# Logits in two groups a block, inputs split at step 6, the first z sum in the transposes' PSUM tile

## The chip, the cores and the metric

The kernel runs on one core of one Trainium2 chip. The metric is the device time of one execution in microseconds (us); a kernel's time is the median of its runs. Five engines work from queues of their own, each strictly in order: PE (TensorE), DVE (VectorE), ACT (ScalarE), POOL (GpSimd) and SP (SyncE, which here only issues DMAs). They meet at semaphores.

## What is computed

The reference, cut to what matters, with x of 8 x 3072 x 256:

```python
X = np.fft.fft(np.fft.fft(x, axis=1), axis=2).real.reshape(24576, 256)
x = (X @ w_a) * (X @ w_b) @ w_out                  # 256 -> 1536 -> 256
logits = x @ phi                                   # 32 slots
d = softmax(logits, over the tokens)
slots = d.T @ x                                    # 32 x 256
out_slots = relu(slots @ w1[e]) @ w2[e]            # 8 experts, 4 slots each
out = softmax(logits, over the slots) @ out_slots
```

## The kernel before

The program has three stages. `_fft` does the Fourier transforms and prepares the weights. `_main` runs from about 215 us to 1555 us of the profile and is the stage that the change touches; it ends in `tail`, which works out the slots. `_out` multiplies the second softmax with the slots' results and stores 24 MB.

`_main` goes through 24 **blocks** (index k) of 1024 tokens. A block has 12 **steps** (index p, the code's `ft`), one for every 128 of the 1536 hidden features; n = 12 k + p counts all 288. The order on every engine is the order in which this Python code issues the instructions; no scheduler moves anything.

What one step issues, by the lines of the profile:

- `layer1(n)`: twelve fp32r matmuls of 512 columns on PE (L531 to L533), six into the PSUM tiles `s`, six into `d`, each of which exists once. DVE adds a correction to the two `s` (L547, twice) and forms sums and a difference with `d` (L552 to L554). ACT copies one `d` (L551). POOL does the rest: a difference (L556) and two products (L557, L558) that give the tile `g`; in every third block (k % 3 == 2) also a copy of one column (L561). `s_sb`, `pl` and `db` have two buffers each, `g` six.
- `transp(n - 2)`: eight PE transposes of the `g` of two steps ago into the PSUM tile `t` (L579), which ACT copies out to `ring` (L582). `t` exists once, so the next transposes wait for that copy.
- In steps 1, 5 and 9 a **group**: `logits` of four `g` tiles (L590, into `l_ps`), then one `z_part` (L599), a sum of the previous block's `ring` tiles weighted by its exponentials. DVE adds the sum to `acc` (L602). The `z` sums, the transposes `y_ps`, `x_ps` and `c_ps` of the softmax steps and some first-block work share one PSUM tile, `x`.

Softmax work on the previous block is spread over the steps by a table: 

```python
    side = {3: ["d"], 4: ["ct"], 5: ["cm", "sum", 0], 9: ["cs", 1], 10: ["co"]}
```

`"cm"` forms exponentials of the logits over the slots (DVE L643 and L644, ACT L645), `"cs"` normalises them (DVE L650, ACT L651, DVE L652 and L653), `"co"` transposes the result (L658) and SP stores it. `"sum"` is a DVE reduction of the other softmax's exponentials (L625) and a small ACT instruction (L626). A number is a `z_part`: 0 in step 5, 1 in step 9; the third is issued in step 1 of the block after.

In step 9 the next block's inputs are split for the fp32r matmuls (`split_eo`): ACT rounds them to `eoh` (L516), DVE subtracts that from them to give the rest `eol` (L519, an instruction with two inputs of 1024 elements in SBUF). SP loads a block's inputs (L507, L508); its queue also carries the stores of `"co"`, the loads of the last stage's weights `w1` and `w2` during the last block, and one load of `wo` (1.5 MB) at step 12.

## Time and profile before

| | us |
|---|---|
| median of 3 runs | 1669.15 (1666.14 to 1671.22) |
| the profiled execution, its time | 1664.62 |
| its span, first to last instruction | 1662.6 |
| PE busy | 1598.5 (96%) |
| DVE busy | 1391.2 (84%) |
| POOL busy | 1146.9 (69%) |
| ACT busy | 640.8 (39%) |

A timeline row of the profile reads: start in us from the span's start, duration in us, engine, line, operation, the tile written and the tiles read, shapes, and xN for N neighbouring instructions of one kind that were merged; in brackets the idle time of the engine before it and what ended it. Matmul durations overlap, so PE is read from start to start. The trace records each fp32 matmul of L590 and L599 twice.

### The profile page before, as it was taken

Reading aid. Unit: us, or ns where it says so; the run is one execution under the profiler, and the core shown is the slowest. Engines: PE = TensorE matmul, PEld = TensorE weight load, DVE = VectorE, ACT = ScalarE, POOL = GpSimd, SP = SyncE. Lnnn points to the kernel's source line nnn. Section 1 sums busy time; section 2 is a strip of 40 time slices with the busy share of each in tenths; the row PEclk is TensorE's granted clock in tenths of the full one; section 3 lists DMA queues with packets and bytes.
Section 4 is the critical chain, followed back from the end, with each engine's and each line's share of the span. In section 5 each row is a group of like instructions: output and inputs, shape, how many; then the busy total and the mean of one; then the engine's idle time right before and its main releaser. Section 6 shows DMA issues by size and latency. Waiting matters only on the chain.

```text
span 1662.6 us, 28294 instructions
## 1 busy us (share of the span) xinstructions
PE 1598.5 (96%) x10837; PEld 1166.9 (70%) x10837; DVE 1391.2 (84%) x2055; ACT 640.8 (39%) x990; POOL 1146.9 (69%) x992
## 2 busy tenths in 40 slices
PE   5999999999999999999999999999999999999985
PEld 3555578777777777777777777777777777777554
DVE  8999889888888888888888988888888888888633
ACT  1322324434434444434343443433443434434343
POOL 1000069888878887888788778877887788878421
PEclk9999999999999999999999999999999999999975
DMA  9777330000000000000000000000000000002689
GB/s 392 271 249 243 106 98 20 23 1 23 24 23 1 23 23 23 1 23 23 23 1 23 23 20 4 23 23 16 8 23 23 1 23 23 23 1 94 281 338 385
DMA packets 34095, 123.71 MB, mean 74 GB/s; under 512 B 3780, under 2 KB 12035, under 8 KB 26792
## 3 DMA queue, kind: packets, MB, share of 16 engines
q1 hardware_dynamic: 28796, 113.98, 18.7%
q10 hardware_dynamic: 5164, 7.92, 1.3%
q8 instruction: 86, 1.41, 0.4%
q14 instruction: 49, 0.40, 0.1%
HBM read 79.36 MB, written 42.52 MB: 73 GB/s over the span
## 4 chain that ended last, share of the span: by engine, by line
PE 81%; DVE 11%; DMA 4%; issue 2%; ACT 1%; POOL 0%; DVEq 0%; ACTq 0%; SPq 0%
PE t_ps L579 14%; PE s L531 8%; PE d L531 8%; PE d L533 8%; PE d L532 8%; PE s L533 7%; PE s L532 7%; PE l_ps L590 7%; PE z_ps L599 6%; PE pt L262 4%; DMA out_dram<-o 3%; DVE eol L519 2%; PE pt L171 1%; DVE f L269 1%; DVE e L276 1%
## 5 line engine op out<-in xcount | busy, mean ns | idle before, releaser
L556 POOL TENSOR_TENSOR db<-s_sb,db 128x512 f32<-128x512 f32 x287 | 373.0, 1300 | 249.7 <-DVE s_sb L553 99.1
L547 DVE SCALAR_TENSOR_TENSOR s_sb<-ub,w,s 128x512 f32<-128x512 f32 x576 | 404.4, 743 | 72.0 <-PE s L533 69.8
L551 ACT COPY db<-d 128x512 f32<-128x512 f32 x288 | 169.7, 589 | 626.7 <-PE d L533 608.7
L557 POOL TENSOR_TENSOR g<-pl 128x512 f32<-128x512 f32 x288 | 384.9, 1336 | 7.7 <-DVE pl L554 6.9
L558 POOL TENSOR_TENSOR g<-s_sb,db 128x512 f32<-128x512 f32 x287 | 372.4, 1298 | 0.0
L582 ACT COPY ring<-t_ps 128x1024 f32<-128x1024 f32 x286 | 290.5, 1016 | 63.8 <-PE t_ps L579 63.8
L579 PE MATMUL t_ps<-ident,g 128*128 128x128 f32 x2296 | 297.3, 272 | 0.0
L579 PEld LDWEIGHTS t_ps<-ident,g 128*128 128x128 f32 x2296 | 268.3, 140 | 39.3 <-issue 0.4
L531 PE MATMUL s<-eoh,wt 128*128 128x512 f32 x576 | 252.6, 438 | 2.4 <-DVE s_sb L547 2.4
L531 PE MATMUL d<-eoh,wt 128*128 128x512 f32 x576 | 226.9, 394 | 3.1 <-DVE s_sb L553 3.1
L533 PE MATMUL d<-eoh,wt 128*128 128x512 f32 x576 | 227.2, 394 | 0.0
L533 PE MATMUL s<-eoh,wt 128*128 128x512 f32 x576 | 226.5, 393 | 0.0
L532 PE MATMUL s<-eol,wt 128*128 128x512 f32 x576 | 225.2, 391 | 0.0
L532 PE MATMUL d<-eol,wt 128*128 128x512 f32 x576 | 225.1, 391 | 0.0
L553 DVE TENSOR_TENSOR s_sb<-s_sb,d 128x512 f32<-128x512 f32 x288 | 197.8, 687 | 9.9
L554 DVE TENSOR_TENSOR pl<-s_sb,d 128x512 f32<-128x512 f32 x288 | 197.5, 686 | 0.5 <-ACT db L551 0.5
L552 DVE TENSOR_TENSOR pl<-s_sb,d 128x512 f32<-128x512 f32 x288 | 195.6, 679 | 0.0
L531 PEld LDWEIGHTS s<-eoh,wt 128*128 128x128 f32 x576 | 108.4, 188 | 76.1 <-issue 28.9
L590 PE MATMUL l_ps<-g,m_sb 128*32 128x256 f32 x2304 | 139.2, 382 | 0.0
L599 PE MATMUL z_ps<-ring,d_sb 128*32 128x512 f32 x1152 | 136.7, 592 | 0.0
L531 PEld LDWEIGHTS d<-eoh,wt 128*128 128x128 f32 x576 | 108.2, 188 | 30.7 <-DVE s_sb L553 7.6
L533 PEld LDWEIGHTS s<-eoh,wt 128*128 128x128 f32 x576 | 108.1, 188 | 25.0
(186 smaller groups left out, 1699.5 us busy)
## 6 DMA issues: line engine op xcount, KB each, us to landing
out_dram<-o SPq DMA_DIRECT2D x23, 1024.0 KB
xt<-in_x_dram SPq DMA_DIRECT2D x15, 1536.0 KB
eoraw<-eo_c SPq DMA_DIRECT2D x16, 512.0 KB
w2t<-in_moe_w_dram SPq DMA_DIRECT2D x4, 2048.0 KB
w1t<-in_moe_w_dram SPq DMA_DIRECT2D x3, 2048.0 KB
eo<-so SPq DMA_DIRECT2D x16, 256.0 KB
eoraw<-eo SPq DMA_DIRECT2D x8, 512.0 KB
ub<-eo_c SPq DMA_DIRECT2D x16, 256.0 KB
```

The lines of the kernel that those rows point to most:

```text
L531: nc.tensor.matmul(ps_, wt[ft // 4][:, ft % 4, 0, e, ab], h[:, e], start=True, stop=False)
L532: nc.tensor.matmul(ps_, wt[ft // 4][:, ft % 4, 0, e, ab], l[:, e], start=False, stop=False)
L533: nc.tensor.matmul(ps_, wt[ft // 4][:, ft % 4, 1, e, ab], h[:, e], start=False, stop=True)
L547: nc.vector.scalar_tensor_tensor(out=s_sb[:, ab], in0=ub, scalar=w128[:, ab, ft:ft + 1], in1=s_ps[ab], op0=ALU.mult, op1=ALU.add)
L553: nc.vector.tensor_tensor(am, s_sb[:, 0], d_ps[0], ALU.subtract)
L556: eng.tensor_tensor(bm, s_sb[:, 1], db, ALU.subtract)
L557: nc.gpsimd.tensor_tensor(g[:, 0:512], pl[:, 0], pl[:, 1], ALU.mult)
L558: eng.tensor_tensor(g[:, 512:1024], am, bm, ALU.mult)
L579: nc.tensor.transpose(t_ps[:, z], g[:, z * P:z * P + P], ident)
L582: nc.scalar.copy(dst, t_ps)
L590: nc.tensor.matmul(l_ps[k][NS * c:NS * c + NS], m_sb[:, ft], g[:, 256 * c:256 * c + 256], start=(ft == 0), stop=(ft == NFT - 1))
L599: nc.tensor.matmul(z_ps[NS * c:NS * c + NS], d_sb[:, hh, NS * c:NS * c + NS], ring[:, :, 2 * c + hh, :], start=(hh == 0), stop=(hh == 1))
```

## The change

- `logits` are issued in two groups a block: five tiles in step 6 and seven in step 1 of the next block. So that the tiles live long enough `g` has nine buffers; the 12 KB for them come from `wo`, which is no tile of its own any more but three loads into `g` buffers, two in the last step and one in `tail`.
- In step 6 the group stands ahead of the step's transposes, behind the `d` matmuls; in step 1 it stands behind the transposes as before. Both `z` sums 0 and 1 are issued in step 6, one behind the other. Sum 0 takes the PSUM tile `t`, sum 1 the tile `x`.
- The next block's inputs are rounded on ACT in step 5 (`split_h`) and the rest is formed on DVE in step 6 (`split_l`), between `"cm"` and the first `z` sum's addition to `acc`. `"cs"` moves from step 9 to step 6, behind that addition; `"co"` from step 10 to step 8.
- The sum of the exponentials is taken by ACT's exponential itself (`accum_out`), and the DVE reduction L625 is gone.

Line numbers of the changed kernel are higher by one from `layer1` on; L513 and L519 are the two halves of the split there.

```diff
-    gp = ctx.enter_context(tc.tile_pool(reuse_waits="tile", name="m_g", bufs=6))
+    gp = ctx.enter_context(tc.tile_pool(reuse_waits="tile", name="m_g", bufs=9))
...
-            nc.scalar.activation(dt_, l_sb, ACTF.Exp, bias=bm[:, 1:2])
+            nc.scalar.activation(dt_, l_sb, ACTF.Exp, bias=bm[:, 1:2], accum_out=al[:, 1:2])
...
-            nc.vector.tensor_reduce(out=al[:, 1:2], in_=s["dt"], axis=AX.X, op=ALU.add)
...
-    side = {3: ["d"], 4: ["ct"], 5: ["cm", "sum", 0], 9: ["cs", 1], 10: ["co"]}
+    side = {3: ["d"], 4: ["ct"], 5: ["h"], 6: ["cm", "sum", "l", 0, "cs", 1], 8: ["co"]}
...
-                z_part(k, v)
+            elif k >= 0:
+                z_part(k, v, "x" if v else "t")
...
+    def load_wo(q):
+        t = gp.tile([P, 1024], F32, tag="g", name="wo").rearrange("p (t d) -> p t d", t=4)
+        nc.sync.dma_start(t, wof[:, 4 * q:4 * q + 4])
+        wo.append(t)
...
-            if p == 9 and k + 1 < nblk:
-                split_eo(k + 1)
...
-        if n >= 2:
+        if n >= 2 and p != 6 and n <= nper:
             rest = transp(n - 2)
...
-        if n % 4 == 1 and 1 < n < nper:
-            for z in range(5, 1, -1):
+            for z in range(7, 1, -1):
                 logits(n - z)
-        if k > 0 and p == 1:
+        if p == 1 and k > 0:
+            for z in range(8 if n < nper else 2, 1, -1):
+                logits(n - z)
...
+        if p == 6:
+            for z in range(6, 1, -1):
+                logits(n - z)
+        if n == nper - 1:
+            load_wo(0)
+            load_wo(1)
...
+        if p == 6:
+            transp(n - 2)
```

What stands in a row on PE in the middle of the program, before: the end of a step 9, its transposes and its group, and the first matmuls of step 10 (`eoh`, `eol` are the inputs, `wt` the weights, `m_sb` the matrix from hidden features to logits, `d_sb` the exponentials).

```order
L532 MATMUL d_8456<-eol,wt 128x512
L533 MATMUL d_8456<-eoh,wt 128x512
L579 MATMUL t_ps<-ident,g 128x128 x8
L590 MATMUL l_ps<-g,m_sb 32x256 x16
L599 MATMUL z_ps<-ring,d_sb 32x512 x8
L531 MATMUL s_8528<-eoh,wt 128x512
L532 MATMUL s_8528<-eol,wt 128x512
```

And on PE after the change, the end of a step 6 and the beginning of step 7:

```order
L533 MATMUL d_8086<-eol,wt 128x512
L534 MATMUL d_8086<-eoh,wt 128x512
L591 MATMUL l_ps<-g,m_sb 32x256 x20
L600 MATMUL z_ps<-ring,d_sb 32x512 x16
L580 MATMUL t_ps<-ident,g 128x128 x8
L532 MATMUL s_8178<-eoh,wt 128x512
L533 MATMUL s_8178<-eol,wt 128x512
```

The group moved ahead of the transposes, and it holds five tiles' logits and two `z` sums in place of four and one.

On DVE before, the end of step 5 with its softmax work and the beginning of step 6:

```order
L554 TENSOR_TENSOR pl<-s_sb,d_7457 128x512
L643 TENSOR_REDUCE cm<-x_ps 128x8
L644 TENSOR_TENSOR ce<-x_ps,cm 128x256
L625 TENSOR_REDUCE al<-dt 128x1
L602 SCALAR_TENSOR_TENSOR acc<-acc,al,z_ps 128x512
L547 SCALAR_TENSOR_TENSOR s_sb<-ub,w_85,s_7527 128x512
```

On DVE before, four steps later, the end of step 9 and the beginning of step 10:

```order
L554 TENSOR_TENSOR pl<-s_sb,d_7648 128x512
L519 TENSOR_TENSOR eol<-eoraw,eoh 128x1024
L650 TENSOR_REDUCE cs<-ce 128x8
L652 RECIPROCAL cs<-cs 128x8
L653 TENSOR_TENSOR ce<-ce,cs 128x256
L602 SCALAR_TENSOR_TENSOR acc<-acc,al,z_ps 128x512
L547 SCALAR_TENSOR_TENSOR s_sb<-ub,w_85,s_7719 128x512
```

On DVE after the change, the end of step 6 and the beginning of step 7:

```order
L555 TENSOR_TENSOR pl<-s_sb,d_7487 128x512
L643 TENSOR_REDUCE cm<-x_ps 128x8
L644 TENSOR_TENSOR ce<-x_ps,cm 128x256
L519 TENSOR_TENSOR eol<-eoraw,eoh 128x1024
L603 SCALAR_TENSOR_TENSOR acc<-acc,al,z_ps 128x512
L650 TENSOR_REDUCE cs<-ce 128x8
L652 RECIPROCAL cs<-cs 128x8
L653 TENSOR_TENSOR ce<-ce,cs 128x256
L603 SCALAR_TENSOR_TENSOR acc<-acc,al,z_ps 128x512
L548 SCALAR_TENSOR_TENSOR s_sb<-ub,w_85,s_7578 128x512
```

The two pieces of DVE work became one; the subtraction L519 stands where L625 stood, directly ahead of the first addition to `acc`, and steps 5 and 9 hold nothing but their own five instructions.

## Rows read from the trace of the kernel before

**Rows 1.** The page: busy time of each engine, share of the span, instructions.
```profile
PE 1598.5 (96%) x10837; PEld 1166.9 (70%) x10837; DVE 1391.2 (84%) x2055; ACT 640.8 (39%) x990; POOL 1146.9 (69%) x992
```

**Rows 2.** The page: the chain that ended last, shares by engine.
```profile
PE 81%; DVE 11%; DMA 4%; issue 2%; ACT 1%; POOL 0%; DVEq 0%; ACTq 0%; SPq 0%
```

**Rows 3.** Timeline of PE: a step 5 with its group, block 10; last, tail.
```profile
792.81 0.48 PE L531 MATMUL s<-eoh,wt 128*128 128x512 f32 x1
...
795.66 1.04 PE L579 MATMUL t_ps<-ident,g 128*128 128x128 f32 x8
796.63 1.93 PE L590 MATMUL l_ps<-g,m_sb 128*32 128x256 f32 x32
798.38 1.90 PE L599 MATMUL z_ps<-ring,d_sb 128*32 128x512 f32 x16
800.21 0.50 PE L531 MATMUL s<-eoh,wt 128*128 128x512 f32 x1
...
1563.93 3.64 PE L599 MATMUL z_ps<-ring,d_sb 128*32 128x512 f32 x32
```

**Rows 4.** Timeline of PE: first matmuls of steps 10, 11 and 0, block 3.
```profile
425.84 0.50 PE L531 MATMUL s<-eoh,wt 128*128 128x512 f32 x1
...
430.18 0.50 PE L531 MATMUL s<-eoh,wt 128*128 128x512 f32 x1 [0.22 <-DVE s_sb L547]
...
434.46 0.48 PE L531 MATMUL s<-eoh,wt 128*128 128x512 f32 x1
```

**Rows 5.** Timeline of PE: the same three matmuls in block 11.
```profile
875.26 0.50 PE L531 MATMUL s<-eoh,wt 128*128 128x512 f32 x1
...
879.13 0.48 PE L531 MATMUL s<-eoh,wt 128*128 128x512 f32 x1
...
882.77 0.48 PE L531 MATMUL s<-eoh,wt 128*128 128x512 f32 x1
```

**Rows 6.** Timeline of DVE: the split's subtraction in blocks 3, 9, 11 and 19.
```profile
423.11 4.34 DVE L519 TENSOR_TENSOR eol<-eoraw,eoh 128x1024 fp32r<-128x1024 f32 x1 [0.26 <-ACT eoh L516]
...
760.17 1.82 DVE L519 TENSOR_TENSOR eol<-eoraw,eoh 128x1024 fp32r<-128x1024 f32 x1 [0.26 <-ACT eoh L516]
...
872.53 1.22 DVE L519 TENSOR_TENSOR eol<-eoraw,eoh 128x1024 fp32r<-128x1024 f32 x1 [0.26 <-ACT eoh L516]
...
1321.89 4.32 DVE L519 TENSOR_TENSOR eol<-eoraw,eoh 128x1024 fp32r<-128x1024 f32 x1 [0.25 <-ACT eoh L516]
```

**Rows 7.** Timeline of POOL: beside the first two of these (blocks 3 and 9).
```profile
418.82 1.32 POOL L556 TENSOR_TENSOR db<-s_sb,db 128x512 f32<-128x512 f32 x1
...
422.57 1.32 POOL L556 TENSOR_TENSOR db<-s_sb,db 128x512 f32<-128x512 f32 x1
...
425.04 1.32 POOL L558 TENSOR_TENSOR g<-s_sb,db 128x512 f32<-128x512 f32 x1
...
760.84 2.29 POOL L557 TENSOR_TENSOR g<-pl 128x512 f32<-128x512 f32 x1
```

**Rows 8.** The line L653: count, duration ns min/median/max.
```profile
L653 DVE TENSOR_TENSOR ce<-ce,cs x24: 424/482/1016, 314.7 to 1577.7; 128x256 f32<-128x256 f32 x24
```

**Rows 9.** Timelines of DVE and POOL: step 5 of block 10.
```profile
797.94 0.41 DVE L625 TENSOR_REDUCE al<-dt 128x1 f32<-128x256 f32 x1
...
796.59 1.29 POOL L556 TENSOR_TENSOR db<-s_sb,db 128x512 f32<-128x512 f32 x1
```

**Rows 10.** Timelines of PE and POOL: step 5 of block 11, one with L561.
```profile
849.54 0.48 PE L531 MATMUL s<-eoh,wt 128*128 128x512 f32 x1
...
849.95 1.30 POOL L556 TENSOR_TENSOR db<-s_sb,db 128x512 f32<-128x512 f32 x1
...
853.95 1.29 POOL L556 TENSOR_TENSOR db<-s_sb,db 128x512 f32<-128x512 f32 x1
```

**Rows 11.** Stretches: busy us (instructions) by engine, clock, DMA share, GB/s.
```profile
1547.00:1551.00 4.00, 4.00 (x24) 2.44 (x17) 2.71 (x5) 0.00 (x0) 2.76 (x3) 1.00 0.00 0
...
1559.00:1583.00 24.00, 21.08 (x203) 9.51 (x199) 9.02 (x25) 6.95 (x20) 1.77 (x2) 1.00 1.01 418
```

More of the change, by code (lines that the diff above doesn't have):

```diff
@@ L509, in load_eo, with split_h, split_l @@
         eo_t[k] = [raw, ub]
-    def split_eo(k):
-        raw, ub = eo_t[k]
-        l = eh.tile([P, 2, 512], F32R, tag="eol", name="eol")
-        h = eh.tile([P, 2, 512], F32R, tag="eoh", name="eoh")
-        if k:
-            nc.scalar.copy(h, raw)
-        else:
-            nc.vector.tensor_copy(h, raw)
+    def split_h(k):
+        h = eh.tile([P, 2, 512], F32R, tag="eoh", name="eoh")
+        (nc.scalar.copy if k else nc.vector.tensor_copy)(h, eo_t[k][0])
+        eo_t[k].append(h)
+    def split_l(k):
+        raw, ub, h = eo_t[k]
+        l = eh.tile([P, 2, 512], F32R, tag="eol", name="eol")
         nc.vector.tensor_tensor(l, raw, h.bitcast(F32), ALU.subtract)
@@ L522, in _main @@
     load_eo(0)
-    split_eo(0)
+    split_h(0)
+    split_l(0)
     nper = nblk * NFT
@@ L565, in transp @@
         k, ft = divmod(n, NFT)
-        g = g_t[n]
+        g = g_t.pop(n) if ft == 4 else g_t[n]
         if ft % 4 == 0:
@@ L585, in logits @@
         k, ft = divmod(n, NFT)
-        g = g_t[n] if n == nper - 1 else g_t.pop(n)
+        g = g_t[n]
         if ft == 0:
@@ L661, in soft_step @@
             nc.sync.dma_start(csc[:, k], ct)
-    side = {3: ["d"], 4: ["ct"], 5: ["cm", "sum", 0], 9: ["cs", 1], 10: ["co"]}
+    side = {3: ["d"], 4: ["ct"], 5: ["h"], 6: ["cm", "sum", "l", 0, "cs", 1], 8: ["co"]}
     def run_side(k, items):
         for v in items:
-            if isinstance(v, str):
+            if v in ("h", "l"):
+                if k + 2 < nblk:
+                    (split_h if v == "h" else split_l)(k + 2)
+            elif k >= 0 and isinstance(v, str):
                 soft_step(k, v)
-            else:
-                z_part(k, v)
+            elif k >= 0:
+                z_part(k, v, "x" if v else "t")
     ex = {}
@@ L739, in tail @@
         soft_step(k, "sum")
+        load_wo(2)
         load_w2(0)
@@ L785, in slots_b @@
             for c in range(4):
-                nc.tensor.matmul(sip[NS * c:NS * c + NS], zt[q][:, c], wo[:, 4 * q + c],
+                nc.tensor.matmul(sip[NS * c:NS * c + NS], zt[q][:, c], wo[q][:, c],
                                  start=(q == 0), stop=(q == 2))
@@ L864, in _main @@
                                 axis=AX.X, op=ALU.add)
-    wo = wpool.tile([P, NFT, D], F32, name="wo")
+    wo = []
     nc.vector.memset(m_run[0], -3.0e38)
@@ L874, in _main @@
             layer1(n)
-            if p == 9 and k + 1 < nblk:
-                split_eo(k + 1)
             if n < 9:
                 extra(n)
-            if n == NFT:
-                nc.sync.dma_start(wo, wof)
-        if n == nper + 1:
-            for z in range(5, 1, -1):
-                logits(n - z)
-        if n >= 2:
+        if n >= 2 and p != 6 and n <= nper:
             rest = transp(n - 2)
@@ L887, in _main @@
             z_part(nblk - 2, 2)
-        if n % 4 == 1 and 1 < n < nper:
-            for z in range(5, 1, -1):
+            for z in range(7, 1, -1):
                 logits(n - z)
-        if k > 0 and p == 1:
+        if p == 1 and k > 0:
+            for z in range(8 if n < nper else 2, 1, -1):
+                logits(n - z)
             soft_step(k - 1, "l")
@@ L896, in _main @@
                     z_part(k - 2, 2)
-        if k > 0 and n < nper:
+        if p == 6:
[4 more added lines that the diff above has]
+            load_wo(1)
+        if n == nper + 1:
+            rest = transp(n - 2)
+        if n < nper:
             run_side(k - 1, side.get(p, []))
+        if p == 6:
+            transp(n - 2)
         if k == nblk - 1 and p in ahead:
```

## The prediction

> **What bounds the kernel now.** I read the page first: PE is busy for 96% of the span and holds 81% of the chain that ended last [rows 1, 2]. DVE, at 84%, has little room, POOL some. So a gain must come out of PE's own sequence or out of the places where PE waits. For these I read PE's timeline from one step's first `s` matmul to the next one's, over all 24 blocks. A plain step takes 3.64 us (879.13 to 882.77, [rows 5]); a step with a group takes 7.40 (792.81 to 800.21, [rows 3]). PE waits in one place only: in nine of the 24 blocks steps 10 and 11 are long. In block 3 they take 4.34 and 4.28 us [rows 4], in block 11 3.87 and 3.64 [rows 5]: 1.11 us lost, 10.0 us in the nine blocks.
>
> The cause stands on DVE. The subtraction L519 takes 1.22 us where POOL is between two instructions (872.53, [rows 6]). In the nine blocks it takes 4.3 us (423.11 is the first, 1321.89 the ninth, [rows 6]). Beside the first, POOL runs L556, L557 and L558 back to back until 425.04 + 1.32 = 426.36, and L519 ends at 427.45, 1.09 later [rows 6, 7]. In seven blocks like block 9 it ends after 1.82 us, and there POOL's next instruction is the one that is stretched, to 2.29 us [rows 6, 7]. So the two engines exclude each other, and when L519 comes while POOL is busy there is a **draw**: won at POOL's next boundary, or lost until POOL runs dry. Of 16 draws 9 were lost; in the remaining seven splits, those of blocks with L561, DVE came first.
>
> **Parts that save.** 1. The stalls in steps 10 and 11 go, as nothing but the usual five DVE instructions is left in step 9: 9 x 1.11 = 10.0 us. If the split in its new place stalls PE again, that is priced below.
>
> 2. Fewer groups. A group adds 7.40 - 3.64 = 3.76 us. Its logits take 1.75 (796.63 to 798.38, four tiles, 0.44 each); a second `z` sum behind a first adds 3.64 - 1.90 = 1.74 [rows 3]. That leaves 3.76 - 1.75 - 1.74 = 0.27 us for going in and out. Tiles and sums stay the same in number; three groups a block become two. In the new group the logits follow the `d` matmuls and the transposes follow `z`, two orders that the trace of before doesn't show, so its going in and out lies between 0 and twice 0.27; I take 0.16, nearer to the measured 0.27 than to the ends and below it because the transposes lead into the next `s` as in a plain step. Saved per block: 2 x 0.27 - 0.16 = 0.38, with the tail's merged group 24 times: 9.1 us (bounds 0 and 13.0).
>
> 3. Costed at nothing. The removed reduction (0.41 us, [rows 9]) was in a step where DVE waited for PE. The accumulator's price on ACT has no row; it lies between nothing and the 0.41 of the instruction that it replaces, on an engine that is 39% busy [rows 1], two steps ahead of its first reader. The rounding on ACT moves into step 5 between two copies; a step's ACT work stays under 3.64 us. SP: the store of `"co"` and the loads queued behind it are issued two steps earlier, the inputs are needed four steps earlier; with nine steps (33 us) left for 0.75 MB that hides. The load of `wo`: two thirds go out when the DMA engines are idle (1547 to 1551, share 0.00); the last third is ahead of `w2` in a stretch that is full (1.01, 418 GB/s, [rows 11]), so `w2` lands 0.52 MB / 418 GB/s = 1.25 us later. That is the bound if PE has no slack there; I take 0.
>
> Without new stalls: 1664.6 (the profiled execution's time) - 10.0 - 9.1 = **1645.5 us**.
>
> **The part that costs: the split in step 6.** The second addition doesn't matter, the first does. The transposes of step 6 need the tile `t`, which holds `z` sum 0 until DVE's L603 has read it, and L603 now stands behind L519. Times from the step's first `s` matmul:
>
> - PE: the transposes of before stood at +2.85 (795.66 - 792.81, [rows 3]). The logits take their place: five tiles, 2.19; two `z` sums, 3.48; with half of the 0.27 the transposes want to start at +8.65.
> - DVE: L625 came at +5.13 (797.94 - 792.81) in step 5; L519 comes there in step 6.
> - POOL: L556 at +3.78 in step 5 [rows 9]. Its cycle is 422.57 - 418.82 = 3.75 us [rows 7], PE's step 3.64, so one plain step later +3.89. The three instructions last to 3.79 after that (426.36 - 422.57): POOL is dry at +7.68. L519 always meets it busy.
> - A lost draw: L519 ends at 7.68 + 1.09 = +8.77, L603 0.74 later at +9.51: PE stalls 0.86 us. Won at the first or the second boundary (+5.2, +6.4), it ends by +7.5, and L603 is done before +8.65: no stall.
> - Blocks with L561: POOL's cycle is 4.00 (849.95 to 853.95), L556 was at +4.41 in step 5 [rows 10], hence at +4.77; dry at +8.56, L519 done at +9.65, L603 at +10.39: 1.74 us. Before, these blocks had no draw; now they have one.
>
> Block 0 has no `z` sum, so at most 15 x 0.86 + 7 x 1.74 = **25.1 us**. With the share lost before, 9 of 16, it is 14.1: 1645.5 + 14.1 = **1659.6**. That share is a weak number. The 24 runs of the shorter two-input instruction L653 never took over 1.02 us [rows 8], less than one POOL instruction (1.3) and itself: they never lost. And L519 will come within 0.1 us of a boundary in most blocks, where before it came 0.8 ahead. The same timing also repeats every three blocks, so draws go together, and the sum can be far from its middle.
>
> The median of before is 4.5 us above the profiled execution; four more lost draws would give that, but no timed run shows it. I carry no offset in the middle and half of it in the upper end.
>
> **Rivals.**
>
> *All draws won (first come, first served).* The waiting engine gets in when the running POOL instruction ends: L519 is done by +7.5, with L561 at 6.06 + 1.09 = +7.15, and PE never stalls: 1645.5, or 1650 with the offset. For it: seven of 16 draws, and L653. Against it: the nine that waited past two more POOL instructions though they came first [rows 6, 7]. The Trainium skill, "SBUF — State Buffer", section "Who interferes with whom", states this rule: a DVE instruction with two SBUF inputs contends with a GpSimd instruction that reads SBUF, the one that issued first holds the shared pair for its whole length and the other blocks until it is done. The trace agrees on the exclusion and disagrees on the order, by the 4.3 us of L519.
>
> *Nearly all draws lost.* One mechanism: L519 waits for POOL's queue to run dry, ahead of L603, which holds `t`. Price 25.1 us: 1670.6, and with the offset 1675, slower than before. It decides from 19.1 / 25.1 = 76% of the price paid; less is a gain.
>
> *The new group is as dear as its bounds.* If going in and out costs 0.54, part 2 is gone: 1659.6 + 9.1 = 1669, no change.
>
> *POOL becomes the bound.* Steps 7 to 11 have no group now. In every third block POOL falls behind by 4.00 - 3.64 = 0.36 us a step, five steps, and then by 0.11 in steps 0 and 1 of the next: 1.8 to 2.0 us, where before it was 0.63 by step 5 (4.41 - 3.78, [rows 9, 10]). If all that reached PE: 7 x 2.0 = 14 us, 1674; I expect none of it, as `g` is needed two steps after it is begun and step 1's group lets POOL catch up; half of it would give 1667.
>
> **How the numbers follow.** Forecast, draws mixed: 1660, its own range 1651 to 1665, chance 0.45. All won 0.22; nearly all lost 0.15; group as dear 0.10; POOL the bound 0.08. A measurement here can tell about 0.3% from no change, so faster is below 1664.1 and slower above 1674.2. Faster: 0.40 of the forecast, 0.22 all won, 0.04 of the last two: 0.66. Slower: 0.08, half of the case of lost draws with the offset and a little of POOL's. Within 0.3%: 0.26. The range reaches from just above all won, 1647, to all lost with half the offset, 1673.
>
> **What would show it.** Steps 10 and 11 at 3.64 in all blocks (step 8 at 3.87) shows part 1. Step 1 at 8.7 and step 6 at 9.4 to 9.5 where L519 is short shows part 2. L519 near 1.2 to 2.4 us with no idle PE ahead of the transposes of step 6 is a draw won; L519 at 3.6 to 4.5 us with step 6 at 10.3 (11.2 with L561) is one lost. The forecast is wrong if L519's length doesn't decide the length of step 6, if steps 7 to 1 are long in blocks with L561, or if `tail` waits for `wo` or `w2`.

## The result and the profile after

The changed kernel takes 1648.26 us (median, 1646.63 to 1651.03), the kernel before 1669.64 (1666.14 to 1671.22) beside it: a ratio of 0.988, interval 0.986 to 0.989, 21.4 us less. The forecast was 1660 (1647 to 1673): the sign is right and the time lies in the range, near its lower end, but the gain is more than twice the 9 us that lay between the forecast and the 1669.15 of before. The profiled execution took 1647.84 with a span of 1645.8, against 1664.62 and 1662.6 before.

The page of the kernel after, busy time by engine and the shares of the chain that ended last [rows 1, 2]:

```profile
PE 1583.5 (96%) x10837; PEld 1165.0 (71%) x10837; DVE 1360.3 (83%) x2031; ACT 643.8 (39%) x1014; POOL 1154.2 (70%) x992
...
PE 84%; DVE 8%; DMA 4%; issue 2%; ACT 1%; POOL 1%; ACTq 0%; SPq 0%; DVEq 0%; POOLq 0%
```

PE is the bound as before. DVE's 24 reductions are gone, and its share of the chain fell from 11% to 8%.

Timeline of PE after, block 3: the first `s` matmul of step 6, the last `d` matmul, the group, the transposes, and the first matmuls of steps 7 and 8 (the answer to [rows 3]):

```profile
401.83 0.47 PE L532 MATMUL s<-eoh,wt 128*128 128x512 f32 x1
...
404.44 0.40 PE L534 MATMUL d<-eoh,wt 128*128 128x512 f32 x1
404.76 2.37 PE L591 MATMUL l_ps<-g,m_sb 128*32 128x256 f32 x40
406.94 3.62 PE L600 MATMUL z_ps<-ring,d_sb 128*32 128x512 f32 x32
410.49 1.09 PE L580 MATMUL t_ps<-ident,g 128*128 128x128 f32 x8
411.34 0.48 PE L532 MATMUL s<-eoh,wt 128*128 128x512 f32 x1
...
414.98 0.48 PE L532 MATMUL s<-eoh,wt 128*128 128x512 f32 x1
```

Step 6 takes 411.34 - 401.83 = 9.51 us, step 7 takes 3.64, and no row has idle time in brackets. All of blocks 2 to 22 read like this, 55.25 us each, within 0.01. By steps, in us, from PE's timeline (first `s` matmul to first `s` matmul), a block without a lost draw on either side (step 0 is left out, 3.64 in both):

| step | 1 | 2 | 3 | 4 | 5 | 6 | 7 | 8 | 9 | 10 | 11 | block |
|---|---|---|---|---|---|---|---|---|---|---|---|---|
| before | 7.40 | 3.66 | 3.85 | 3.85 | 7.38 | 3.66 | 3.63 | 3.64 | 7.40 | 3.88 | 3.64 | 55.62 |
| forecast | 8.7 | | | | | 9.4 to 9.5 | | 3.87 | | 3.64 | 3.64 | |
| after | 8.69 | 3.67 | 3.86 | 3.85 | 3.63 | 9.51 | 3.64 | 3.86 | 3.63 | 3.64 | 3.64 | 55.25 |

The subtraction L519 on DVE after (blocks 3, 5 and 7; [rows 6]), behind the first of them the addition L603 that holds the transposes:

```profile
406.94 1.22 DVE L519 TENSOR_TENSOR eol<-eoraw,eoh 128x1024 fp32r<-128x1024 f32 x1
408.91 0.75 DVE L603 SCALAR_TENSOR_TENSOR acc<-acc,al,z_ps 128x512 f32<-128x512 f32 x1 [0.76 <-PE z_ps L600]
...
517.43 2.09 DVE L519 TENSOR_TENSOR eol<-eoraw,eoh 128x1024 fp32r<-128x1024 f32 x1
...
627.93 2.40 DVE L519 TENSOR_TENSOR eol<-eoraw,eoh 128x1024 fp32r<-128x1024 f32 x1
```

And POOL beside the first of them [rows 7]:

```profile
405.73 1.29 POOL L557 TENSOR_TENSOR db<-s_sb,db 128x512 f32<-128x512 f32 x1
406.96 2.33 POOL L558 TENSOR_TENSOR g<-pl 128x512 f32<-128x512 f32 x1
```

Of 23 draws none was lost. In 13 blocks L519 came 0.07 to 0.09 us ahead of the end of a POOL instruction (405.73 + 1.29 = 407.02) and was let in at once: it took 1.22, and POOL's next instruction was the one that was stretched (2.33). In one block it took 1.43, in the seven with L562 (the copy of one column, L561 before) up to 2.34, and in two it missed the boundary next to it and took the one after (2.40). In block 3 the addition waits for PE and ends at 408.91 + 0.75 - 401.83 = 7.83 us into the step, ahead of the transposes at 8.66, as the prediction had it for a draw won.

**Where the time went.** The last step of the program starts at 1552.04 before and at 1531.04 after: 21.0 us gained. They are 10.0 of the nine stalls, 0.37 in each of the 21 blocks 2 to 22 (7.8), and 3.2 in blocks 0, 1 and 23 (52.67 became 50.22 in block 0, as the logits of three of its tiles moved on into block 1). The span is only 16.8 shorter: the tail gave back 4.2. Timeline of PE in the tail, before:

```profile
1555.76 1.04 PE L573 MATMUL t_ps<-ident,g 128*128 128x128 f32 x8
1556.73 1.92 PE L599 MATMUL z_ps<-ring,d_sb 128*32 128x512 f32 x16
1558.47 1.91 PE L590 MATMUL l_ps<-g,m_sb 128*32 128x256 f32 x32
1560.31 1.09 PE L579 MATMUL t_ps<-ident,g 128*128 128x128 f32 x8
1562.30 0.44 PE L630 MATMUL y_ps<-ident,dt 128*128 128x128 f32 x2 [0.90 <-ACT dt L620]
...
1563.67 0.27 PE L747 MATMUL mp<-ident,l_run 128*1 128x128 f32 x1 [0.82 <-ACT l_run L626]
```

And after:

```profile
1534.76 0.60 PE L574 MATMUL t_ps<-ident,g 128*128 128x128 f32 x4
1535.90 0.33 PE L574 MATMUL t_ps<-ident,g 128*128 128x128 f32 x1 [0.54 <-POOL g L559]
1536.49 0.55 PE L574 MATMUL t_ps<-ident,g 128*128 128x128 f32 x3 [0.26 <-POOL g L562]
1536.97 1.92 PE L600 MATMUL z_ps<-ring,d_sb 128*32 128x512 f32 x16
1538.71 3.21 PE L591 MATMUL l_ps<-g,m_sb 128*32 128x256 f32 x56
1541.85 1.09 PE L580 MATMUL t_ps<-ident,g 128*128 128x128 f32 x8
1543.93 0.44 PE L630 MATMUL y_ps<-ident,dt 128*128 128x128 f32 x2 [0.99 <-ACT dt L621]
...
1545.30 0.37 PE L757 MATMUL mp<-ident,l_run 128*1 128x128 f32 x1 [0.82 <-ACT l_run L626]
1545.61 5.12 PE L600 MATMUL z_ps<-ring,d_sb 128*32 128x512 f32 x32
```

Stretches of after behind these waits (length, busy time by engine, granted clock, DMA share, GB/s):

```profile
1545.60:1547.40 1.80, 1.80 (x13) 0.48 (x16) 0.64 (x2) 0.67 (x2) 0.00 (x0) 0.50 0.98 387
1547.40:1550.60 3.20, 3.20 (x28) 0.67 (x20) 1.45 (x4) 0.00 (x0) 0.00 (x0) 0.81 0.78 266
```

Before, the transposes L573 (L574 after) went through without a wait from 1555.76 to 1556.73; now they take 2.21, 1.24 more, with PE waiting for POOL. Seven tiles' logits take 3.14 instead of 1.84 for four (1.30, moved here, not lost). The two `z` sums L600 take 5.12 instead of 3.64 (1.48 more): the granted clock is 0.50 there, its lower level of 1.2 GHz, behind two waits of 0.99 and 0.82. Before, waits of 0.90 and 0.82 stood there too, and the `z` sums behind them ran at a clock of 1.00 [rows 3, 11]. 1.24 + 1.30 + 1.48 = 4.0 of the 4.2.

The slower clock is not a fixed price of the change. Timelines of PE, the same `z` sums in two runs of the experiments below: the kernel before with two tiles swapped, with the old waits (0.90 and 0.82), and the kernel after with two instructions put in on DVE, with the new ones (0.99 and 0.82).

```profile
1565.09 5.33 PE L599 MATMUL z_ps<-ring,d_sb 128*32 128x512 f32 x32
...
1545.27 3.64 PE L600 MATMUL z_ps<-ring,d_sb 128*32 128x512 f32 x32
```

The granted clock in their first 1.8 us is 0.51 and 1.00. Of all twenty traces the `z` sums were slow in five of the eight that have the tail of after and in two of the other twelve.

### The profile page after: what moved, and what is told of

The parts are those of the page before. It is cut to its first block, busy times and chain, and to the rows that moved or that the text cites. A ratio compares the mean times of both kernels' runs of the same rounds, so it can differ in the third digit from the quotient of the medians.

```text
span 1645.8 us, 28203 instructions
## 1 busy us (share of the span) xinstructions
PE 1583.5 (96%) x10837; PEld 1165.0 (71%) x10837; DVE 1360.3 (83%) x2031; ACT 643.8 (39%) x1014; POOL 1154.2 (70%) x992
## 4 chain that ended last, share of the span: by engine, by line
PE 84%; DVE 8%; DMA 4%; issue 2%; ACT 1%; POOL 1%; ACTq 0%; SPq 0%; DVEq 0%; POOLq 0%
PE t_ps L580 15%; PE s L532 8%; PE d L534 8%; PE l_ps L591 8%; PE s L534 8%; PE s L533 8%; PE d L533 8%; PE d L532 8%; PE z_ps L600 8%; DMA out_dram<-o 2%; PE pt L262 2%; DVE f L269 1%; DVE e L276 1%; DMA wu<-in_moe_w_b_dram 1%; DVE dz L284 1%
## 5 line engine op out<-in xcount | busy, mean ns | idle before, releaser
L558 POOL TENSOR_TENSOR g<-pl 128x512 f32<-128x512 f32 x288 | 396.7, 1377 | 0.5 <-DVE xl L684 0.3
L591 PE MATMUL l_ps<-g,m_sb 128*32 128x256 f32 x2304 | 134.2, 381 | 0.0
L600 PE MATMUL z_ps<-ring,d_sb 128*32 128x512 f32 x1152 | 133.9, 598 | 0.0
L533 PEld LDWEIGHTS d<-eol,wt 128*128 128x128 f32 x576 | 108.1, 188 | 24.9
```

What stands on the lines that cost most here:

```text
L533: nc.tensor.matmul(ps_, wt[ft // 4][:, ft % 4, 0, e, ab], l[:, e], start=False, stop=False)
L558: nc.gpsimd.tensor_tensor(g[:, 0:512], pl[:, 0], pl[:, 1], ALU.mult)
L591: nc.tensor.matmul(l_ps[k][NS * c:NS * c + NS], m_sb[:, ft], g[:, 256 * c:256 * c + 256], start=(ft == 0), stop=(ft == NFT - 1))
L600: nc.tensor.matmul(z_ps[NS * c:NS * c + NS], d_sb[:, hh, NS * c:NS * c + NS], ring[:, :, 2 * c + hh, :], start=(hh == 0), stop=(hh == 1))
```

## The experiments

"Lost" is a draw as in [rows 6, 7]: DVE waits past two more POOL instructions and takes 4.25 us or more. "Alone" below is the split alone moved, the first experiment. "Row" is explained where it is first needed. Times of single runs are good to some 4 us (twelve runs of the kernel before lay between 1663.5 and 1671.2).

**The split moved alone.** In the kernel before, `split_eo` became the two halves of the kernel after, the rounding in step 5 and the subtraction in step 6; the two tiles of the split are also claimed in the other order, which a run further down undoes.

```diff
-            if p == 9 and k + 1 < nblk:
-                split_eo(k + 1)
+            if p == 6 and k + 1 < nblk:
+                split_l(k + 1)
```

> The kernel before with the split alone moved: rounding on ACT in step 5, subtraction on DVE in step 6, groups in steps 1, 5 and 9 as before. The stalls of steps 10 and 11 go (10 us). The subtraction follows DVE's own instructions here, without waiting for ACT, 0.7 us ahead of POOL's boundary, about as far as before (0.75 to 0.79). Theory A' (far ahead of a boundary is a toss, close to it is won): about half of the 23 draws lost, each making step 7 some 2.1 us and step 8 some 0.4 us longer: 1655 + 12 x 2.5 = 1685 us. Theory C (a subtraction that comes straight behind another DVE instruction wins its first boundary, one that has waited for ACT tosses): none lost, step 8 at 3.9, 1656 to 1658 us.

1661.83 us, ratio 0.998 [0.997, 0.999]. Duration of L519 in ns, min/median/max:

```profile
L519 DVE TENSOR_TENSOR eol<-eoraw,eoh x24: 1226/1823/1830, 212.1 to 1472.2; 128x1024 fp32r<-128x1024 f32 x24
```

All 23 draws were won (1.82 us each). Steps 10 and 11 are at 3.88 and 3.64 in every block, but step 8 is at 3.88 where it was 3.64: even a draw won in a plain step costs PE 0.24 us two steps on, some 5.8 us in all. Theory A' is out; theory C has the draws right and the time 4 us too low, and further down a run in which L519 comes straight behind a DVE instruction and loses 13 draws refutes it. So moving the split is worth less than the stalls it ends, unless a group stands beside it.

**The change with the split left in step 9.** Groups, `"cs"`, `"co"` and the accumulator as after.

```diff
-    side = {3: ["d"], 4: ["ct"], 5: ["h"], 6: ["cm", "sum", "l", 0, "cs", 1], 8: ["co"]}
+    side = {3: ["d"], 4: ["ct"], 6: ["cm", "sum", 0, "cs", 1], 8: ["co"]}
...
+            if p == 9 and k + 1 < nblk:
+                split_h(k + 1)
+                split_l(k + 1)
```

> The changed kernel with the split put back into step 9, rounding and subtraction, as it was; the two groups, the normalisation and both z sums stay in step 6. Step 9 has no group now that could cover it. Won at the first boundary: step 11 at 3.9, 55.3 us a block, 1649 us. Lost: step 10 at 5.8 to 6.4 and step 11 at 4.3, 2.5 to 3.2 us a block. With 9 of 16 lost, as before, and blocks with the extra copy as well: about 1680 us. So this tells what the two groups are worth alone: -9 us if draws are won, a loss of 10 us or more if half of them are lost.

1659.88 us, ratio 0.996 [0.994, 0.998]. No draw was lost here either, although L519 waits for ACT as it did before. Step 11 is 0.25 longer in plain blocks, and steps 10 and 11 are 0.11 and 0.64 longer in blocks with the extra copy. That is 11 us above what was expected for draws won. In the traces the last step starts 10.8 us later than in the kernel after (1541.85 against 1531.04; the medians, from different calls, are 11.6 apart), so the subtraction beside the group of step 6 is worth about that.

**The subtraction twice.** In the kernel after, L519 issued two times in a row.

```diff
-        nc.vector.tensor_tensor(l, raw, h.bitcast(F32), ALU.subtract)
+        for _ in range(2 if k else 1):
+            nc.vector.tensor_tensor(l, raw, h.bitcast(F32), ALU.subtract)
```

> The changed kernel with the subtraction of the split issued twice in a row (same result); block 0's inputs once. It forces what a lost draw would have cost: the first z sum's addition, and with it the PSUM tile that the transposes of step 6 wait for, comes 1.1 us later or, where POOL gets in between, 2.4 us later. By the prediction's working step 6 grows from 9.51 to between 10.4 and 11.5 us and no other step changes: 1648 + 22 x 1.0 to 2.0 = 1670 to 1692 us. If the position of that addition does not matter, step 6 stays at 9.5 and steps 7 and 8 take the delay, or none does.

1679.36 us. Step 6 alone grows, to 10.10 to 11.29, by 30.8 us in all. PE's transposes of step 6 in block 3 wait for the first addition (L604 here):

```profile
414.90 1.09 PE L581 MATMUL t_ps<-ident,g 128*128 128x128 f32 x8 [1.70 <-DVE acc L604]
```

That settles the price: what ends late ahead of the first addition is paid by PE.

**The kernel before once more.**

> The kernel before, unchanged, profiled a second time. Theory A (a draw is decided by timing of tens of ns that a program repeats): nine of 16 draws lost again, in the same blocks, 1660 to 1667 us. Theory B (a coin for each draw, not tied to the program): another number of lost draws, 4 to 14 of 16, in other blocks; each lost one makes steps 10 and 11 together 1.1 us longer.

1671.01 us, 12 draws lost: in eight of the nine blocks of the first time and in four others. At 1.1 us each, three more are 3.3 of the 6.4 us between the two executions: about half of this difference is the number of lost draws.

**Is it the distance from POOL's boundary?** One DVE instruction of one column ahead of L519 in the kernel before:

```diff
+        if k:
+            pad = p1.tile([P, 1], F32, tag="pad", name="pad")
+            nc.vector.tensor_scalar_mul(pad, h.bitcast(F32)[:, 0, 0:1], 1.0)
```

> The kernel before with one more DVE instruction ahead of the subtraction L519 in step 9 (one column of the rounded inputs copied to a spare tile; it waits for ACT's rounding as L519 did, so L519 comes about 0.1 us later, about 0.65 us ahead of POOL's boundary instead of 0.755 to 0.789). Theory 1, the distance from POOL's boundary decides a draw: at most 3 of the 16 draws are lost, L519 takes about 1.75 us in plain blocks, steps 10 and 11 are at 3.9 and 3.65, and the time is that of before in this call less 9 to 12 times 1.1 us, so 10 to 13 us less. Theory 2, the place in step 9 tosses the draw whatever the distance: 8 to 12 of 16 are lost (steps 10 and 11 at 4.3), and the time is that of before within 3 us.

1667.74 us, ratio 0.999 [0.998, 1.001]. Ten draws were lost, at 0.63 to 0.67 us ahead of POOL's next start; the distance theory failed. In two runs of the kernel after L519 was held back to POOL's second boundary, in the second of them to the distance at which it had lost before:

```diff
+            if k < nblk - 1:
+                pad = p1.tile([P, 8], F32, tag="pad", name="pad")
+                nc.vector.tensor_reduce(out=pad, in_=x_ps, axis=AX.X, op=ALU.max)
```

> The kernel after with the reduction of cm repeated into a spare tile ahead of L519 in step 6 (about 0.45 us of DVE), so that L519 misses the first boundary of POOL by 0.4 us and comes about 0.85 us ahead of the second. Theory 1, distance decides: few or no draws are lost, L519 takes about 1.9 us, and steps 6 stay at 9.5; the time is that of after within 2 us. Theory 2, each draw is a toss at 9 in 16: about half of the plain blocks have L519 at 3 us or more and step 6 at 10.3 to 10.4, the time is 8 to 14 us above after.

and in the second also

```diff
+                nc.vector.tensor_scalar_mul(pad[:, 0:1], m_run[0], 1.0)
```

> As the run with the repeated reduction, and one more small DVE instruction of one column behind it, so that L519 comes about 0.76 us ahead of POOL's second boundary, the distance at which it lost in the kernel before. Theory 1, distance decides: most draws of the 15 plain blocks are lost, L519 takes about 3.2 us there, step 6 is at 10.3 to 10.5, and the time is 8 to 14 us above that of the run with the reduction alone. Theory 2, a toss whatever the distance: the same number of lost draws as with the reduction alone, give or take four.

1650.79 and 1646.00 us. In plain blocks L519 came 0.92 to 0.94 and 0.73 to 0.76 us ahead and won every time; step 6 is at 9.52 in both. The second run is against the distance again; the toss at 9 in 16 failed too.

**Is it the addresses, the wait for ACT, or the step?** Three runs: the two tiles of the split claimed in the other order in the kernel before; the same swap undone in "alone"; and "alone" with rounding in step 8 and subtraction in step 9.

```diff
-        l = eh.tile([P, 2, 512], F32R, tag="eol", name="eol")
         h = eh.tile([P, 2, 512], F32R, tag="eoh", name="eoh")
+        l = eh.tile([P, 2, 512], F32R, tag="eol", name="eol")
```

> The kernel before with one thing changed: in the split the tile of the rounded inputs (eoh) is claimed ahead of that of the rest (eol), as in the kernel after, so that the two tiles change places in SBUF; every instruction and its order stay. Theory A, the addresses decide: no draw is lost in step 9, steps 10 and 11 are at 3.9 and 3.65 in all blocks, 10 to 13 us less than before in this call. Theory B, step 9 with its group decides (the addresses don't matter): 8 to 12 of 16 draws are lost and the time is that of before within 3 us.

```diff
     def split_h(k):
+        l = eh.tile([P, 2, 512], F32R, tag="eol", name="eol")
         h = eh.tile([P, 2, 512], F32R, tag="eoh", name="eoh")
```

> The kernel with the split alone moved (rounding in step 5, subtraction in step 6), which lost no draw of 23, with the tiles claimed in the order of the kernel before (eol ahead of eoh). Theory A, the addresses decide: about half of the 15 plain draws of step 6 are lost, L519 takes 3 to 4.3 us there and step 7 or 8 is longer by about 1 us, 8 to 12 us more than the 1661.8 of the kernel with the split alone. Theory B, the place decides: no lost draw, 1662 within 3.

```diff
-            if p == 6 and k + 1 < nblk:
+            if p == 9 and k + 1 < nblk:
                 split_l(k + 1)
...
-        if n < nper and p == 5 and k + 1 < nblk:
+        if n < nper and p == 8 and k + 1 < nblk:
             split_h(k + 1)
```

> The kernel with the split alone moved, but the rounding in step 8 and the subtraction back in step 9, the step with a group, straight behind L555 with no wait for ACT; tiles claimed as in the kernel after. Theory A, the addresses decide: no draw lost, about 1662. Theory B, step 9 with its group decides: 8 to 12 of 16 plain draws lost with L519 at 4.3 us, about 1669. Theory C, the wait for ACT and the group together decide: no draw lost.

1667.10 us (ratio 0.998 [0.997, 0.999]) with 11 lost; 1662.36 with none; 1667.35 with 13 lost of 16, though L519 waited for nothing (later expectations say 14). The loss belongs to step 9 of the old arrangement, not to the addresses and not to the wait.

**The group, or the DVE work behind L519?** In the kernel before `"cs"` moved to step 8; in "alone" `"cs"` put behind L519 in step 6; in "alone" both halves one step ahead of where they were, rounding in 4 and subtraction in 5; and the last of the three above with `"cs"` in step 10 and `"co"` in 11.

```diff
-    side = {3: ["d"], 4: ["ct"], 5: ["cm", "sum", 0], 9: ["cs", 1], 10: ["co"]}
+    side = {3: ["d"], 4: ["ct"], 5: ["cm", "sum", 0], 8: ["cs"], 9: [1], 10: ["co"]}
```

> The kernel before with the normalisation "cs" moved from step 9 to step 8, so that L519 in step 9 is followed on DVE by the z sum's addition L602, which waits for PE; the group stays in step 9 on PE. Theory F, a draw is lost where DVE's next instruction is ready at once (L650, as in the kernel before): no draw is lost, steps 10 and 11 at 3.9 and 3.65, 10 us or more below the run of before beside it. Theory G, PE's group in step 9 decides: 8 to 14 of 16 draws are lost, L519 at 4.3 us.

```diff
-    side = {3: ["d"], 4: ["ct"], 5: ["cm", "sum", 0], 9: ["cs", 1], 10: ["co"]}
+    side = {3: ["d"], 4: ["ct"], 5: ["cm", "sum", 0], 6: ["cs"], 9: [1], 10: ["co"]}
```

> The kernel with the split alone moved to step 6, and "cs" moved behind it in step 6, so that L650, ready at once, follows L519; no group in that step. Theory F: about half of the draws or more are lost and L519 is at 3 us or more. Theory G: none is lost, L519 at 1.82 us, and the time is that of the split moved alone, 1662 within 3.

```diff
-            if p == 6 and k + 1 < nblk:
+            if p == 5 and k + 1 < nblk:
                 split_l(k + 1)
...
-        if n < nper and p == 5 and k + 1 < nblk:
+        if n < nper and p == 4 and k + 1 < nblk:
             split_h(k + 1)
```

> The kernel with the split alone moved, with the rounding in step 4 and the subtraction in step 5, a step that has a group and DVE work behind the subtraction that is ready (L644, "cm"). Theory H, a draw is lost where both stand in its step, a group on PE and DVE work ready behind L519: half or more of the plain draws are lost, L519 at 4.3 us or more, steps 6 and 7 longer by 1.1 us. Theory S, only step 9 of the kernel before does it (its cs, or where it stands in the block): no lost draw.

```diff
-    side = {3: ["d"], 4: ["ct"], 5: ["cm", "sum", 0], 9: ["cs", 1], 10: ["co"]}
+    side = {3: ["d"], 4: ["ct"], 5: ["cm", "sum", 0], 9: [1], 10: ["cs"], 11: ["co"]}
```

> The kernel with the rounding in step 8 and the subtraction in step 9, of which 14 of 16 draws were lost, with "cs" moved to step 10 and "co" to step 11, so that only the addition to acc, which waits for PE, follows L519; the group stays. Theory H, both are needed: no draw lost, L519 at 2.1 us or less. Theory G, the group on PE alone does it: 8 or more lost, L519 at 4.3 us or more. Step 10 gets longer in either case, as cs has no group beside it there.

1657.59, 1692.11, 1684.45 and 1679.11 us, with 0, 0, 0 and 14 draws lost. Neither the group nor the work behind L519 is it, nor both. (In the first, 15 blocks had no draw, as DVE came ahead of POOL.) The times carry another lesson: 1.65 us a block more than an undisturbed block of before in the second, where `"cs"` follows a won L519 in a plain step and DVE is late for step 7 and 8, and 1.4 in the third, where `"cm"` and the sum stand between L519 and the addition to `acc`.

**POOL's unbroken row.** What the lost draws share is on POOL. Timeline of POOL in the run with 13 lost, block 4, steps 6 to 9, and L519 there on DVE:

```profile
466.83 1.31 POOL L557 TENSOR_TENSOR db<-s_sb,db 128x512 f32<-128x512 f32 x1 [3.64 <-DVE s_sb L554]
468.09 1.31 POOL L558 TENSOR_TENSOR g<-pl 128x512 f32<-128x512 f32 x1
469.34 1.30 POOL L559 TENSOR_TENSOR g<-s_sb,db 128x512 f32<-128x512 f32 x1
470.58 1.32 POOL L557 TENSOR_TENSOR db<-s_sb,db 128x512 f32<-128x512 f32 x1
...
478.10 1.31 POOL L557 TENSOR_TENSOR db<-s_sb,db 128x512 f32<-128x512 f32 x1
479.34 1.31 POOL L558 TENSOR_TENSOR g<-pl 128x512 f32<-128x512 f32 x1
480.57 1.31 POOL L559 TENSOR_TENSOR g<-s_sb,db 128x512 f32<-128x512 f32 x1
...
478.31 4.66 DVE L519 TENSOR_TENSOR eol<-eoraw,eoh 128x1024 fp32r<-128x1024 f32 x1
```

POOL waits once, ahead of step 6 (3.64 in brackets), and then each instruction starts 30 to 100 ns ahead of the end of the one before it. L519 meets the tenth of that row, waits for it and two more, and ends 1.1 us after the twelfth. Counted in this way (a row ends where an instruction starts later than 20 ns ahead of its predecessor's end; the limit was set after the runs), all draws of all traces fall into two classes:

| POOL instruction that L519 meets | traces | draws | lost |
|---|---|---|---|
| the 10th of its row | before, the same again, with the pad, with the tiles swapped, in step 9 with rounding in 8, the same with "cs" in 10 | 90 | 69 (9, 12, 10, 11, 13, 14) |
| the 1st to 8th | these and all others | 359 | 0 |

(The ninety are 15 in each of six traces; the sixteenth draw of each, in block 0, met the 7th of a row and was won.) The second class hangs on that limit. Timeline of POOL after, block 3, the last product of step 4 and the first difference of step 5:

```profile
400.66 1.29 POOL L559 TENSOR_TENSOR g<-s_sb,db 128x512 f32<-128x512 f32 x1
401.96 1.30 POOL L557 TENSOR_TENSOR db<-s_sb,db 128x512 f32<-128x512 f32 x1
```

The second starts 5 ns behind the end of the first, which counts as the end of a row; L519 meets the fourth from there. If only idle time of 25 ns or more ended a row, most plain draws of the kernel after would be at the 13th, 16.3 us into POOL's work, and with the two pads at the 14th, and all of them were won. So the length of POOL's work without idle time does not decide by itself.

The last run breaks the row and keeps step 9: the run with 13 lost, with POOL's difference left out in step 7.

```diff
-        eng.tensor_tensor(bm, s_sb[:, 1], db, ALU.subtract)
+        if ft != 7:
+            eng.tensor_tensor(bm, s_sb[:, 1], db, ALU.subtract)
```

> The kernel with the rounding in step 8 and the subtraction in step 9 (14 of 16 draws lost), with POOL's difference L557 left out in step 7 of every block, so that a part of the hidden features is not the reference's. The group, L650 and everything else in step 9 stay; POOL has caught up by step 8, and the instruction that L519 meets in step 9 is at most the 4th of an unbroken row of POOL instructions instead of the 10th, with L519 about 0.8 us ahead of its end. Theory R, a draw is lost only when POOL has gone through ten instructions without a wait: no draw lost, L519 at about 1.9 us, steps 10 and 11 at 3.9 and 3.65. Theory S, something else in step 9 does it: 8 or more of the plain draws are lost, L519 over 4 us.

1655.24 us. Timelines of POOL and DVE, the same stretch of block 4:

```profile
470.48 1.30 POOL L559 TENSOR_TENSOR g<-pl 128x512 f32<-128x512 f32 x1 [0.62 <-DVE pl L555]
471.74 1.29 POOL L560 TENSOR_TENSOR g<-s_sb,db 128x512 f32<-128x512 f32 x1
473.33 1.30 POOL L558 TENSOR_TENSOR db<-s_sb,db 128x512 f32<-128x512 f32 x1 [0.30 <-DVE s_sb L554]
...
477.10 1.29 POOL L558 TENSOR_TENSOR db<-s_sb,db 128x512 f32<-128x512 f32 x1
478.34 2.27 POOL L559 TENSOR_TENSOR g<-pl 128x512 f32<-128x512 f32 x1
...
477.54 1.94 DVE L519 TENSOR_TENSOR eol<-eoraw,eoh 128x1024 fp32r<-128x1024 f32 x1
```

POOL waited 0.30 us ahead of step 8, L519 met the fourth instruction of a row, 0.81 us ahead of the next, and all 23 draws were won; step 9 is otherwise as it was. So POOL's past decides, in the one run that tests it, and not the step; which trait of that past it is, the number of instructions, the time or something else, this run does not separate.

**`"cs"` ahead of the first addition.** The kernel after with two entries of the table exchanged.

```diff
-    side = {3: ["d"], 4: ["ct"], 5: ["h"], 6: ["cm", "sum", "l", 0, "cs", 1], 8: ["co"]}
+    side = {3: ["d"], 4: ["ct"], 5: ["h"], 6: ["cm", "sum", "l", "cs", 0, 1], 8: ["co"]}
```

> The kernel after with "cs" (L650 to L653) ahead of the first z sum's addition, directly behind L519. Theory F: L519 loses draws in plain blocks and blocks with L562, 3 us or more long, and step 6 is then at 10.3 or more with cs in front of the addition. Theory G: no lost draw, L519 as in the kernel after (1.22, 2.1 and 2.3 us); step 6 then at 9.5, or up to 9.8 where L519 takes 2.3 us and the 1.3 us of cs come behind it.

1661.26 us. No draw was lost for two boundaries, but of the 14 plain blocks from block 3 on L519 missed the boundary next to it in six and came just behind it in a seventh (two of 14 missed in the kernel after). Timeline of DVE, block 3:

```profile
407.38 2.40 DVE L519 TENSOR_TENSOR eol<-eoraw,eoh 128x1024 fp32r<-128x1024 f32 x1
409.70 0.41 DVE L650 TENSOR_REDUCE cs<-ce 128x8 f32<-128x256 f32 x1
...
411.12 1.39 DVE L603 SCALAR_TENSOR_TENSOR acc<-acc,al,z_ps 128x512 f32<-128x512 f32 x2
```

The addition starts 411.12 - 409.70 = 1.42 us after L650, which has taken its place behind L519, and step 6 is over 10.1 us in 14 of 22 blocks, where the expectation without lost draws had 9.8 at most: 12.4 us in all. The place of the first addition ahead of the normalisation is worth that much in this execution; over half of it comes from the seven plain blocks, and how often a boundary is missed there varies (two, one and two of 14 in three executions with step 6 as in the kernel after).

**The tail in another order**, five tiles' logits and the `z` sum ahead of the transposes that wait for POOL, beside the kernel after unchanged:

```diff
-            z_part(nblk - 2, 2)
-            for z in range(7, 1, -1):
+            for z in range(7, 2, -1):
                 logits(n - z)
+            z_part(nblk - 2, 2)
+            transp(n - 2)
+            logits(n - 2)
```

> The kernel after, unchanged, for comparison on the same chip with the changed tail and for the spread of its draws: 1648 us within 2, no draw lost until POOL ran dry, and the tail's PE at the lower clock for about 3 us behind its z sum and its logits.

> The kernel after with the tail in another order: the logits of five tiles and the last z sum stand ahead of the transposes of the last-but-one tile g, where PE waited 1.24 us for POOL in the changed kernel. If that wait was lost time, and the waits of 0.99 and 0.82 us behind it with the clock at 1.2 GHz came from it, 1.2 to 2.7 us less than the kernel after on the same chip. If the tail is bound by POOL's last product and the softmax behind it, no difference over 0.5 us.

1649.31 us (1649.21 to 1650.16) unchanged and 1647.93 (1645.32 to 1651.39) reordered, ratios to before of 0.989 [0.987, 0.990] and 0.988 [0.986, 0.990]: not told apart. PE of the reordered tail:

```profile
1535.38 2.37 PE L591 MATMUL l_ps<-g,m_sb 128*32 128x256 f32 x40
...
1539.39 1.09 PE L574 MATMUL t_ps<-ident,g 128*128 128x128 f32 x8
...
1543.51 0.44 PE L630 MATMUL y_ps<-ident,dt 128*128 128x128 f32 x2 [1.00 <-ACT dt L621]
...
1545.13 5.34 PE L600 MATMUL z_ps<-ring,d_sb 128*32 128x512 f32 x32
```

The wait for POOL is gone, and from the last step's start (1531.57) to L630 it takes 11.94 us instead of 12.89: 0.95 less. The `z` sums are as slow as in the kernel after (5.34; granted clock 0.51 in the first 1.8 us), so the slower clock doesn't come from that wait.

## Why the prediction was right in sign and too small

- **The stalls** (10.0 us): right. Steps 10 and 11 are at 3.64 in every block.
- **The groups** (0.38 a block, 9.1 in all): 0.37 a block. With the blocks at the ends the whole came to 11.0, of which 1.30 went to the tail with the moved logits: 9.7. The 0.16 for the new group was a choice between 0 and 0.54 that no row of before could decide; by the prediction's subtraction step 6 gives 9.51 - 3.64 - 2.19 - 3.48 = 0.20, so this hit is in part luck.
- **Costed at nothing**: right for the loads of `wo` (PE waits for none) and for the accumulator, which ACT reads out in an instruction of 0.19 us that nothing waits for. The rival of the group as dear as its bounds is out.
- **The price formula**: right. L519's end decides step 6, as the doubled subtraction showed, and in block 3 L519, POOL and the transposes came within 0.02 us of the times that it worked out (+5.13, +3.89, +8.65).
- **The step that failed** is the number of draws that pay: the share of 9 in 16 was carried over from step 9 to step 6, 14.1 us. It was 0 there. The prediction called the share weak and looked at the distance from the boundary; but draws were lost at 0.6 to 1.1 us ahead of POOL's next start in some runs and won at the same distances in others. What separates lost from won in these runs is POOL's past when DVE comes. The difference between the two steps was in the trace of before: POOL's cycle is 3.75 us and a plain step 3.64, as the prediction itself says, so POOL falls back by 0.11 a step and from step 6 to step 9 never waits. In steps 3 and 4 PE takes 3.85, so POOL catches up, and in step 6 L519 meets a row that is short by the limit above.
- **All draws won**, the rival at 0.22, is what happened. Its rule (the Trainium skill, "SBUF — State Buffer", section "Who interferes with whom": the engine that issued first holds the shared pair for the length of its instruction, and the other is blocked until that is done) fits 338 of the 359 draws of the second class, not the 21 that came within 0.1 us of a boundary and were let in one later, and not the 69 that waited for three instructions.
- **POOL as the bound**: it shows only in the tail (1.24 us), where the transposes of the last tiles follow at once.
- **The tail** was left out: 1.24 of a new wait, 1.30 of logits moved into it and, in this execution, 1.48 of slower clock. 1664.6 - 21.0 + 4.2 = 1647.8. The sum without new stalls was 1645.5; the profiled execution lies 2.3 above it, and the wait and the clock are 2.7. Without them the time would have come out at the rival's 1645.5, so that it lies inside the stated range is luck. The profiled execution of before lay 5.0 below its median, with nine lost draws where the repeat had 12; that spread, for which the middle carried no offset, is the rest of the 21.4; about half of it goes with lost draws, as far as the two profiled executions show.

**What stays open.** Why DVE loses against a long row isn't shown, nor why 21 of 90 won there. POOL's lag behind DVE is no better sign: its first instruction of the step starts 0.14 to 0.45 us behind the start of DVE's last one in draws that were lost, and within the same limits in draws of shorter rows, all won. In the kernel after the row is interrupted by a hitch of 3 to 21 ns in most plain blocks, ahead of step 5, and with the pads the instruction there even starts 3 to 18 ns ahead of its predecessor's end, against 31 or more inside a row. That so little is enough is a correlation of some 15 draws in each execution, not a test. Nor is it shown what makes the tail's clock fall in some executions and not in others.

## What to carry to other kernels

Here DVE and POOL excluded each other at a price that depended on the place, so a share of losses read in one place is not a property of the pair. Look at what the other engine has been doing since it last waited; a place behind a step in which that engine idles is worth trying, and in the one run that tested it the losses ended. What a long DVE instruction costs depends on what stands behind it: put the one that releases PE (here the addition to `acc`) directly behind it, beside a group that covers both. And carry the sum past the last step, since work and waits that leave the loop can turn up in the tail.

## What the runs showed that was not expected

- DVE can wait past three POOL instructions though it came 1.05 us ahead of the end of the first: L519 took up to 4.68 us, 1.22 of it its own. It happened 69 times in 90 draws where POOL had gone through nine instructions since a wait of 3 us or more, and never in 359 others.
- The same program lost 9 and 12 draws in two executions, eight of them in the same blocks: about 1.1 us each.
- An instruction that comes within 0.1 us of a boundary is let in there or one boundary later: 12 to 2 in the plain blocks from block 3 on of the kernel after, 7 to 6 with `"cs"` behind it.
- TensorE's clock fell to 1.2 GHz for the `z` sums of the tail (granted 0.50, 5.12 instead of 3.64 us) behind waits of 0.99 and 0.82 us, but not in every run with these waits (it stayed at 1.00 in three of eight), and it fell to 0.51 in one run with the old waits of 0.90 and 0.82.
